# Half products of the first two feature tiles with the first 256 rows from 32-bit operands, row tiles 0 and 1 normalised one by one, and dues set anew, in a spectral filter with a gated feed-forward

## The chip, the cores and the metric

The kernel runs on one core of a Trainium2 chip. The metric is the device time of one execution in microseconds. The engines are PE (matrix products), DVE and ACT (elementwise work), POOL (some elementwise work) and SP, which issues the DMAs. Each engine runs its own instructions in program order; semaphores connect them.

## The reference

```
xn = (x - mean(x)) / sqrt(var(x) + 1e-5)              # x: 2048 x 512
s  = irfft2(rfft2(xn) * (w_r + 1j * w_i))             # w: 2048 x 257
gate, up = xn @ W_gate, xn @ W_up                     # W: 512 x 1376
h  = gate * (gate > 0) * up
g  = silu(h @ W_down)                                 # 1376 x 512
out = x + s * g
```

## The kernel before

**Numbers.** Every 32-bit operand is split into two f16 halves, high and low. A product is three passes over them (`PASSES`: high·high, high·low, low·high), summed in PSUM. So that the halves keep their precision, each weight tile is first scaled by a power of two: ACT squares it and sums along the rows, PE adds over the partitions with a matrix of ones (`group_scale`, into the PSUM tile `small` for groups 0 and 1, into a tile `sum` for the others), DVE makes the scale `p`, and ACT and DVE write the halves `wgu` (`group_split`).

**Tiles.** The 2048 rows are 16 row tiles of 128, taken in pairs c (x0 is row tiles 0 and 1, x1 is 2 and 3), and four blocks of 512 rows for the feed-forward. The 1376 features are 11 feature tiles f, the last of 96. They are loaded in the groups `GROUPS`: f = 0, 1 and 2 alone, then two by two. The raw 32-bit weights of group g are `raw{g}_0` (gate) and `raw{g}_1` (up).

**The feed-forward.** For each block and each f, `product` makes the gate and the up sums (`gu`) of 512 rows: 12 matmuls each (four parts of 128 inputs by three passes). `rectify` makes `r` (ACT, Relu), `hidden` multiplies by the up sums (DVE) and splits the result into the halves `h16`. `down` multiplies them by the split down weights `wds` into `dn`; the scale of these hangs on all weight tiles. `down_scale`: the sums of the raw down weights (ACT) times `rho`, the inverse scales of all groups, give `md`; DVE reduces it, SP writes the 128 results to DRAM as one row (`row_md`) and reads the row back to all partitions (`rows_md`), DVE takes the greatest (`max_md`) and makes the scales `scd`. `down_weights` then makes the halves f by f. The f16 pair of f is written in the place of the raw tile of f − 1, so the high half of f + 1 (ACT) waits for the low half of f (DVE).

**The opening.** The first 512 rows are turned by PE instead of by DMA (`turn_row`): four transposes per row tile into `head` (PSUM), the high half of `xT` by ACT, the low half by DVE. For f = 0 and 1 (`HALF`) of block 0 the product is made in two halves of 256 rows, so that rows 0 to 255 can begin before rows 256 to 511 are there. `keep_busy` puts dummy matmuls of ones into `small` until then.

**The filter.** The two-dimensional transform is done as stages of small matrix products: the first stage `s` per pair of row tiles (with `xs`, folded rows), its result written to DRAM, read back by chunks q, the middle stages `y`, `xx`, `z`, `v`, the filter's weights between `xx` and `z`, DRAM again, and a last stage. These stand on PE between the products of the feed-forward.

**The order.** No order is written out. `Plan` collects steps, each with an engine, a planned cost, what it reads and writes, and for some a due time; dues are handed back to what a step depends on. `Plan.run` then lists the steps by its own clock: of those that can begin, each engine takes the one with the earliest due. The instructions are put out in that order. The numbers at the top of the file set the dues: of the feed-forward through a running clock (`tick`, from `T0`), of the stages by a start and a step (`FIRST`, `MID`, `LAST`), of the down weights by `DOWN`. So a changed number can move work far from where it is used.

Of the kernel before, what the change touches and what calls it, by code (L numbers as in the profile page):

```python
# [14 lines left out]
P = 128  # L15
# [14 lines left out]

T0, DOWN, FIRST, FIRST_STEP, MID, MID_STEP, LAST, LAST_STEP = 1.2, 94.9, 53.3, 17.6, 150.3, 18.1, 292.6, 10.8
LOADS, LOADX = [4.2, 0, 4.4, None, None, None, None], [-2.7, -0.3]
FOLDS, FOLD_LEAD, MARGIN = ['DVE', 'DVE', 'DVE', 'DVE', 'DVE', 'DVE', 'DVE', 'DVE'], 67.8, 1.95
# [5 lines left out]
HURRY, SLOW, SLOW_TO = -2, 1, 20  # L41
LOWS = [("DVE", "DVE")] * 8


RANGES = ((0, 257, 0), (257, 512, 1))
# [189 lines left out]
def kernel(ctx: ExitStack, tc: tile.TileContext, x, wg, wu, wd, wl, ew, sp, c_r, c_d, c_m, c_x, c_s, out):  # L235
# [37 lines left out]
    POOL.memset(unit, 0.0)  # L273
    POOL.affine_select(out=unit, in_=unit, compare_op=ALU.not_equal, fill=1.0, base=0, pattern=[[-1, P]], channel_multiplier=1)
    warm = cpool.tile([P, 1], F32, name="warm")
    ACT.activation(warm, ones[:, 0:1], AF.Sqrt)
    DVE.memset(md, 0.0)

# [23 lines left out]
    def load_x(c):  # L302
        tile_of(f"x{c}", "k4", [P, 2, D], F32)
        if c == 1:
            after_first(("x1", 0), lambda: T["x1"][:, 0, 0:1])
        for i in range(1 + (c == 0)):
            rows = slice(i, i + 1) if c == 0 else slice(0, 2)
            step("SP", .5, lambda rows=rows: SP.dma_start(T[f"x{c}"][:, rows], x[:, 2 * c + rows.start:2 * c + rows.stop, :]),
                 writes=[(f"x{c}", i)], lead=14 if c else None, kb=256 * (rows.stop - rows.start), lag=2.2, due=(LOADX[c] + i * .01) if c < 2 else None)

    def x_names(c, i):
        return [(f"x{c}", 0 if c else i)]
# [1 line left out]
    def stats(c, q, j):  # L314

        def run(i):
            st = T[f"st{c}"][:, 6 * i:6 * i + 6]
            DVE.bn_stats(st, T[f"x{c}"][:, i, :])
            DVE.bn_aggr(T[f"mv{c}"][:, i, :], st)
        tile_of(f"st{c}", "q", [P, 12], F32)  # L320
        tile_of(f"mv{c}", "mv", [P, 2, 2], F32)
        for i in range(2):
            step("DVE", .82, lambda i=i: run(i), reads=x_names(c, i), writes=[(f"st{c}", i), (f"mv{c}", i)])

    def deviation(c):

        tile_of(f"q{c}", "q", [P, 4, 2], F32)

        def first():
            q = T[f"q{c}"]  # L330
            DVE.tensor_scalar(q[:, 0], T[f"mv{c}"][:, :, 1], EPS, -4.0 / XS ** 2, op0=ALU.add, op1=ALU.mult)

        def last():
            ve, sq, y, t = (T[f"q{c}"][:, i, :] for i in range(4))
            DVE.reciprocal(y, sq)
            for i in range(2):
                DVE.scalar_tensor_tensor(t[:, i:i + 1], y[:, i:i + 1], ve[:, i:i + 1], y[:, i:i + 1],
                                         op0=ALU.mult, op1=ALU.mult)
            DVE.scalar_tensor_tensor(y, t, 3.0, y, op0=ALU.add, op1=ALU.mult)
            if "ACT" in NORM[c]:  # L340
                DVE.scalar_tensor_tensor(ve, T[f"mv{c}"][:, :, 0], -1.0, y, op0=ALU.mult, op1=ALU.mult)
        step("DVE", .13, first, reads=[(f"mv{c}", 0), (f"mv{c}", 1)], writes=[f"q{c}"], port=True)
        step("ACT", .11, lambda: ACT.activation(T[f"q{c}"][:, 1], T[f"q{c}"][:, 0], AF.Sqrt, scale=-1.0),
             reads=[f"q{c}"], writes=[(f"q{c}", 1)])
        step("DVE", .78 + .14 * ("ACT" in NORM[c]), last, reads=[(f"q{c}", 1)], writes=[(f"q{c}", 2)], port=True)
        return f"q{c}", 0

    def deviations(cs):

# [16 lines left out]
    def normalise(c, q, at, engines=("DVE", "DVE")):  # L366

        tile_of(f"xf{c}", "k4", [P, 2, D + 2], F32)

        def run(i):  # L370
            to, x = T[f"xf{c}"][:, i, 0:D], T[f"x{c}"][:, i, :]
            if engines[i] == "ACT":
                ACT.activation(to, x, AF.Identity, bias=T[q][:, 0, i:i + 1], scale=at()[:, i:i + 1])
            else:
                DVE.tensor_scalar(to, x, T[f"mv{c}"][:, i, 0:1], at()[:, i:i + 1], op0=ALU.subtract, op1=ALU.mult)
        for i in range(2):
            e = engines[i]
            step(e, .62 if e == "ACT" else dve2(512), lambda i=i: run(i), reads=[*x_names(c, i), (f"mv{c}", i), (q, 2)],
                 writes=[(f"xf{c}", i)], port=e == "DVE")

    def turn(c, lows):
# [24 lines left out]
    def turn_row(c, i):  # L406

        if (c % 2, i) == (0, 0):
            tile_of(f"xT{c // 2}", "xg", [P, 4, 8, P], F16)
        if i == 0:  # L410
            tile_of(f"head{c}", "F", [P, 2, D], F32)
        j = 2 * (c % 2) + i
        head = lambda: T[f"head{c}"][:, i, :]
        xt = lambda h: T[f"xT{c // 2}"][:, j, 4 * h:4 * h + 4].rearrange("p k r -> p (k r)")

        def run():
            for k in range(4):
                cols = slice(k * P, k * P + P)
                PE.transpose(head()[:, cols], T[f"xf{c}"][:, i, cols], unit)
        step("PE", .45, run, reads=[(f"xf{c}", i)], writes=[(f"head{c}", i)])  # L420
# [66 lines left out]
    def load_group(g):  # L487
        w = sum(fwidth(f) for f in GROUPS[g])
        for i, src in enumerate((wg, wu)):
            tile_of(f"raw{g}_{i}", "k4", [P, 4, w], F32)  # L490
            if g == 1 and not i:
                after_first("raw1_0", lambda: T["raw1_0"][:, 0, 0:1])
            of = src[:, 4 * P * GROUPS[g][0]:4 * (P * GROUPS[g][0] + w)].rearrange("p (k f) -> p k f", k=4)
            step("SP", .5, lambda i=i, of=of: SP.dma_start(T[f"raw{g}_{i}"], of),
                 reads=["go"] if g else [], writes=[f"raw{g}_{i}"], lead=12 if g else None, kb=2 * w, lag=2.5, due=LOADS[g])

    def squares(g):
        tile_of(f"m{g}", "m", [P, 4], F32)
# [7 lines left out]

    def group_scale(g):
        nf = len(GROUPS[g])
        if g > 1:
            tile_of(f"sum{g}", "F", [P, 4], F32)  # L510
        to, name = ((lambda: T[f"sum{g}"]), f"sum{g}") if g > 1 else ((lambda: T["small"][:, 4 * g:4 * g + 4]), ("small", g))
# [3 lines left out]
        step("DVE", .52, lambda: scale_of(to()[:, :2 * nf], T[f"p{g}"][:, :, :2 * nf], 9), reads=[name], writes=[f"p{g}"], port=True)  # L515

    def group_split(g):
        fs = GROUPS[g]
# [144 lines left out]

    def tick(cost):
        t = clock[0]
        clock[0] += cost * (SLOW if cost < 2 and t < SLOW_TO else 1.0 if t < 60 else 1.17)
        return t

    def product(c, f, i, rows=slice(0, 4), tag="gu"):
# [10 lines left out]
                tile_of(name, tag, [P, 2, 4, P], F32)  # L680
        elif name not in T.tiles:
            tile_of(name, tag, [P, 4, P], F32)

        def run():
            t, xT = T[name][:, i] if tag == "F" else T[name], T[f"xT{c}"]
# [19 lines left out]
    def rectify(c, f):  # L705
        e, n = fwidth(f), f"r{c}_{f}"
        G, names = sums[c, f, 0]
        tile_of(n, "k2", [P, 4, P], F32)
        step("ACT", act(512), lambda: ACT.activation(T[n][:e], G()[:e], AF.Relu, scale=2.0 ** -22), reads=names, writes=[n], due=clock[0] + 3)

    def hidden(c, f):
# [5 lines left out]
        if f == TAIL:  # L717
            def run():
                for s in range(2):
                    DVE.tensor_mul(h32()[:64, 2 * s:2 * s + 2], up()[64 * s:64 * s + 64, 0:2], r()[:64, 2 * s:2 * s + 2])  # L720
                DVE.tensor_mul(h32()[64:e], gate()[96:], r()[64:e])
            step("DVE", 1.6, run, reads=[*G, *U, f"r{c}_{f}"], writes=[n32], due=clock[0] + 3)
        else:
            step("DVE", dve(512), lambda: DVE.tensor_mul(h32(), up(), r()), reads=[*U, f"r{c}_{f}"], writes=[n32], due=clock[0] + 3)
        step("ACT", act(512), lambda: ACT.activation(h16()[:e, 0], h32()[:e], AF.Copy), reads=[n32], writes=[(n16, 0)])
# [294 lines left out]
    for c in range(NCH):  # L1020
# [7 lines left out]
        for k in [c] if c < 2 else [c - 1, c] if c % 2 else []:  # L1028
# [8 lines left out]
    filter_scale(MID - 12)  # L1037
    for h in range(2):
        for f in range(HALF):
            for i in range(2):  # L1040
                product(0, f, i, slice(2 * h, 2 * h + 2), ("gu", "dn", "F")[f])
            if h:
                rectify(0, f)
                hidden(0, f)
# [12 lines left out]
        ff_steps(c)  # L1057
    for q in range(NCH):
        T.within(f"mid{q}", "mid")
        fft_chunk(q, [MID + MID_STEP * q + k for k in (0, 5, 15, 20)])  # L1060
    T.within(None, None)
    for c in range(NCH):
        last_stage(c, LAST + LAST_STEP * (c | PAIR2))
    for c in range(NCH):
        for i in range(2):
            finish(c, i, LAST + 10 + LAST_STEP * c if c < 6 else clock[0] + 8)
    T.run()


# [120 lines left out]
```

## Time and profile before

| | |
|---|---|
| median of 3 runs | 409.06 us (409.02 to 409.29) |
| span of the profiled execution | 407.1 us |
| PE busy | 401.4 us (99%) |
| DVE busy | 304.0 us (75%) |
| ACT busy | 188.0 us (46%) |
| POOL busy | 46.7 us (11%) |
| granted PE clock | 1.000 |

The profiler saw one execution; of that one the span, from the first to the last instruction, is what it gives for its time. The timed runs have some 2 us more around it. Nearly all records bear the line of one helper (L65 before, L73 after), so groups are told apart by the names of tiles: `gu<-xT,wgu` is a product of the feed-forward, `dn<-wds,h` a down product. A row of the timeline has its start, its busy time, the engine, the line, the operation, out<-in, and how many instructions it gathers.

### The profile page before, as it was taken

What the parts mean: (1) busy time and instruction counts of PE and PEld (TensorE: products, weight loads), DVE (VectorE), ACT (ScalarE), POOL (GpSimd) and SP (SyncE); (2) the same over time, 40 slices, a digit from 0 to 9 for tenths busy, and PEclk for the clock granted to TensorE, in tenths of its full rate; (3) what the DMA queues carried; (4) which work ended last, traced back from release to release, by engine and by line L of the source; (5) the groups of instructions that cost most, each with busy time, mean ns of one, the idle gap of its engine ahead of it and who ended that gap; (6) DMA issues with size and microseconds to landing.
All of it is one profiled execution on the core that took longest, in us unless ns stands there. A gap on an engine that the chain in (4) does not pass through costs nothing.

```text
span 407.1 us, 7606 instructions
## 1 busy us (share of the span) xinstructions
PE 401.4 (99%) x2992; PEld 211.5 (52%) x2992; DVE 304.0 (75%) x647; ACT 188.0 (46%) x358; POOL 46.7 (11%) x72
## 2 busy tenths in 40 slices
PE   8999999999999999999999999999999999999995
PEld 7864444444444445455465455546555444444555
DVE  4897986998798979706987578686792328987974
ACT  4999823743467636222355433534523336242411
POOL 0000000000000000001612032030330008040300
PEclk9999999999999999999999999999999999999999
DMA  7980002218549608690006540324201297563242
GB/s 244 403 304 1 0 2 109 54 52 208 171 152 305 172 15 209 128 291 13 2 0 191 173 144 0 100 92 149 52 2 52 61 242 182 161 185 105 103 156 103
DMA packets 36291, 51.78 MB, mean 127 GB/s; under 512 B 15840, under 2 KB 17600, under 8 KB 36256
## 3 DMA queue, kind: packets, MB, share of 16 engines
q1 hardware_dynamic: 36256, 51.31, 42.5%
q8 instruction: 23, 0.38, 0.4%
q14 instruction: 12, 0.10, 0.1%
HBM read 35.55 MB, written 12.60 MB: 118 GB/s over the span
## 4 chain that ended last, share of the span: by engine, by line
PE 97%; ACT 1%; DVE 1%; issue 0%
PE gu L65 55%; PE dn L65 27%; PE s L65 3%; PE z L65 3%; PE xx L65 3%; PE small L65 2%; PE y L65 2%; PE v L65 2%; PE dn_3b L65 1%; ACT xT L65 1%; ACT wgu L65 0%; PE head L65 0%; DVE xT L65 0%; PE sum L65 0%; DVE p L65 0%
## 5 line engine op out<-in xcount | busy, mean ns | idle before, releaser
L65 PE MATMUL gu<-xT,wgu 128*128 128x512 f16 (+1 forms) x1008 | 213.3, 369 | 0.4 <-DVE xT L65 0.4
L65 PEld LDWEIGHTS <-wgu 128*128 128x128 f16 x1008 | 97.5, 98 | 107.5 <-issue 3.5
L65 PE MATMUL dn<-wds,h 128*128 128x512 f16 (+2 forms) x528 | 115.8, 373 | 0.0
L65 PEld LDWEIGHTS <-h 128*128 128x128 f16 (+1 forms) x561 | 53.7, 98 | 57.3 <-issue 2.0
L65 DVE TENSOR_TENSOR h<-gu,r 128x512 f32<-128x512 f32 (+2 forms) x52 | 33.6, 646 | 24.2 <-PE gu L65 22.9
L65 ACT ACTIVATE h<-h 128x512 f16<-128x512 f32 (+1 forms) x44 | 27.5, 626 | 51.0 <-DVE h L65 51.0
L65 POOL TENSOR_TENSOR po<-tt,tt 128x256 f32<-128x256 f32 x16 | 14.4, 900 | 262.6 <-DVE tt L65 208.7
L65 ACT ACTIVATE r<-gu 128x512 f32<-128x512 f32 (+1 forms) x44 | 26.2, 595 | 36.5 <-PE gu L65 36.3
L65 DVE TENSOR_TENSOR h<-h,h 128x512 f16<-128x512 f32 (+1 forms) x44 | 29.7, 689 | 5.3 <-ACT h L65 5.1
L65 DVE SCALAR_TENSOR_TENSOR tt<-xsp,cw,wt 128x512 f32<-128x512 f32 x32 | 25.3, 847 | 0.0
L65 POOL TENSOR_TENSOR ae<-zz 128x128 f32<-128x128 f32 (+1 forms) x32 | 17.8, 593 | 62.8 <-ACT zz L65 47.9
L65 ACT ACTIVATE g<-dn,cdi 128x512 f32<-128x512 f32 (+1 forms) x16 | 10.6, 673 | 23.9 <-PE dn L65 23.9
L65 PE MATMUL gu<-xT,wgt 128*64 128x256 f16 (+1 forms) x144 | 17.0, 309 | 0.0
L65 DVE TENSOR_TENSOR sv<-sv,g 128x512 f32<-128x512 f32 (+1 forms) x17 | 11.2, 690 | 6.4 <-ACT g L65 6.1
L65 DVE TENSOR_TENSOR t<-v,t 128x1024 f16<-128x1024 f32 x8 | 9.8, 1219 | 7.9 <-ACT t L65 7.9
L65 DVE TENSOR_TENSOR z<-z,z 128x1024 f16<-128x1024 f32 x8 | 9.7, 1218 | 7.5 <-ACT z L65 7.5
L65 ACT ACTIVATE z<-z 128x1024 f16<-128x1024 f32 x8 | 8.2, 1024 | 15.2 <-PE z L65 15.2
L65 POOL TENSOR_TENSOR pf<-tt,tt 128x256 f32<-128x256 f32 x16 | 14.0, 888 | 7.7 <-PE gu L65 7.7
L65 ACT ACTIVATE p<-pf 128x1024 f16<-128x1024 f32 x8 | 8.4, 1056 | 13.0 <-DVE pf L65 13.0
L65 DVE SCALAR_TENSOR_TENSOR wgu<-raw,p,wgu 128x512 f16<-128x512 f32 x20 | 14.4, 745 | 0.1
L65 ACT ACTIVATE xs<-xs 128x1024 f16<-128x1024 f32 x8 | 8.3, 1052 | 12.8 <-DVE xs L65 9.3
L65 ACT ACTIVATE wgu<-raw 128x512 f16<-128x512 f32 x20 | 12.3, 619 | 3.7 <-DMA raw<-in_wg 3.7
(134 smaller groups left out, 430.6 us busy)
## 6 DMA issues: line engine op xcount, KB each, us to landing
A_d<-t SPq DMA_DIRECT2D x16, 256.0 KB, 3.3
rw<-in_wl SPq DMA_DIRECT2D x8, 512.0 KB, 5.1
wt<-in_wl SPq DMA_DIRECT2D x8, 512.0 KB, 4.8
at<-A_d SPq DMA_DIRECT2D x8, 512.0 KB, 4.9
C_d<-t SPq DMA_DIRECT2D x16, 256.0 KB, 3.3
ct<-C_d SPq DMA_DIRECT2D x16, 256.0 KB, 5.6
xt<-in_x SPq DMA_DIRECT2D x16, 256.0 KB, 4.3
out<-xt SPq DMA_DIRECT2D x15, 256.0 KB, 2.1
```

The costliest lines, as they stand in the source:

```text
L65: return lambda *args, **kw: self.tc.keep_in_program_order(f(*args, **kw))
```

## The change

The change has these parts:

- **Row tiles 0 and 1.** `deviation` and `normalise` of pair 0 treat the two row tiles one by one (`ALONE`). The statistics of row tile 1 are made by ACT (a sum, a scaling, a sum of squares) and one DVE multiplication.
- **Transposed rows.** For pair 0 the `head` is first copied as 32-bit numbers to `xTf0` (ACT) and `xTf1` (DVE); the halves of `xT` are made from these copies.
- **32-bit half products.** For f < 2 and rows 0 to 255, `product` multiplies the raw weights by `xTf`: per row tile and part of 128 inputs one matmul of 128 columns, 32 matmuls in all, instead of 48 f16 matmuls of 256 columns. These sums are not scaled, so `rectify` and `hidden` treat the two halves of such a tile apart, with the scale `p` and a new tile `ups` for the first.
- **PSUM.** Group 2 sums its squares into `small`; the second feature tile's halves use a tile of the tag `F`.
- **Dues.** `BUSY` goes from 79 to 42 dummies; the starts and steps of the stages become lists; loads, squares and folds get other leads.

```
-BUSY, LATE, PAIR1, PAIR2 = 79, 0.4, 0, 0
-SQUARES, HALF = 32.82, 2
+BUSY, LATE = 42, 0.4
+SQUARES, HALF = 32.321, 2
+ALONE, EVAC, WHOLE = (((0,), (1,)), ((0, 1),)), ("ACT", "DVE"), .95
+HALVES, HEADS, STATS = ('gu', 'F'), [None, 8.91], ((0, 1),)
...
+            if (c, i) in STATS:
...
+                step("ACT", .75, lambda: ACT.activation(junk(), of(), AF.Copy, accum_out=st()[:, 6:7]),
...
+                step("ACT", .2, lambda: ACT.activation(st()[:, 7:8], st()[:, 6:7], AF.Copy, scale=-1.0 / D),
...
+                step("ACT", .8, lambda: ACT.activation(junk(), of(), AF.Square, bias=st()[:, 7:8], accum_out=st()[:, 8:9]),
...
+                step("DVE", .13, lambda: DVE.tensor_scalar(mv()[:, i, :], st()[:, 6:9:2], 1.0 / D, None, op0=ALU.mult),
...
+        if c == 0:
+            n = f"xTf{i}"
+            tile_of(n, "k2", [P, 4, P], F32)
...
+            step(e, (dve if e == "DVE" else act)(512), act_ if e == "ACT" else lambda: DVE.tensor_copy(T[n].rearrange("p k r -> p (k r)"), head()),
...
+            step("ACT", act(512), lambda: ACT.activation(xt(0), of(), AF.Copy), reads=[n], writes=[(f"xT{c // 2}", j, 0)])
+            step("DVE", dve(512), lambda: DVE.tensor_sub(xt(1), of(), xt(0)), reads=[n, (f"xT{c // 2}", j, 0)],
...
+        if c == 0 and f < HALF and rows.start == 0:
+            def whole(j):
+                for k in range(4):
+                    matmul(to()[:, j], T[f"raw{g}_{i}"][:, k, :], T[f"xTf{j}"][:, k, :], start=k == 0, stop=k == 3)
+            for j in range(2):
+                step("PE", WHOLE, lambda j=j: whole(j), reads=[f"xTf{j}", f"raw{g}_{i}"], writes=[(name, 0, i)], due=tick(WHOLE))
...
+            for k, by in enumerate((lambda: T[f"p{f}"][:, 0, 0:1], lambda: 2.0 ** -22)):
+                at = slice(2 * k, 2 * k + 2)
+                step("ACT", act(256), lambda at=at, by=by: ACT.activation(T[n][:, at], G()[:, at], AF.Relu, scale=by()),
...
-            first_stage(k, FIRST + FIRST_STEP * (k | PAIR1))
+            first_stage(k, FIRSTS[k])
...
-        fft_chunk(q, [MID + MID_STEP * q + k for k in (0, 5, 15, 20)])
+        fft_chunk(q, [MIDS[q] + k for k in STAGES])
```

The order on PE in the opening, before: the two row tiles are turned together (`head`, eight transposes), dummies follow, then the sum for the scale of a weight group (`m,ones`), and the first f16 half product.

```order
L65 MATMUL small<-ones 128x256
L65 MATMUL head_214<-unit,xf_201 128x128 x8
L65 LDWEIGHTS ones
L65 MATMUL small<-ones 128x256
...
L65 MATMUL small<-m_251,ones 128x2
...
L65 LDWEIGHTS wgu_77
L65 MATMUL gu_0_0_274<-xT_233,wgu_77 128x256
```

After, at the same place; row tile 0 was turned a little ahead, and the first row here is the last dummy before the products.

```order
L73 MATMUL small<-ones 128x256
L73 MATMUL gu_0_0_218<-xTf_209,raw_0_129 128x128 x4
L73 MATMUL gu_0_1_231<-xTf_209,raw_1_134 128x128 x4
L73 MATMUL head_197<-unit,xf_157 128x128 x4
L73 MATMUL gu_1_245<-xTf_209,raw_0_153 128x128 x4
L73 MATMUL small<-m_189,ones 128x2
L73 MATMUL gu_0_0_218<-xTf_251,raw_0_129 128x128 x4
...
L73 MATMUL head_293<-unit,xf_274 128x128 x8
L73 MATMUL gu_1_245<-xTf_209,raw_1_166 128x128 x4
...
L73 LDWEIGHTS wgu_77
L73 MATMUL gu_0_0_218<-xT_267,wgu_77 128x256
```

The half products of rows 0 to 255 now stand ahead of the weight sums and the first `wgu`, two of the eight groups even ahead of the turning of row tile 1; the turning of rows 256 to 511 (eight transposes) stands behind six of them.

The order on DVE around the reduction of `md`, before. `p` and `rho` belong to the last weight groups, `h_0_6` is the multiplication in `hidden` of block 0, f = 6, which reads the up sums `gu_6_1`.

```order
L65 SCALAR_TENSOR_TENSOR rho<-p_686 128x2
L65 TENSOR_SCALAR wgu_82<-raw_1_393,p_659 128x4x128
L65 TENSOR_TENSOR md<-md,rho 128x11
L65 TENSOR_REDUCE md<-md 128x1
L65 SCALAR_TENSOR_TENSOR wgu_82<-raw_1_393,p_659,wgu_82 128x4x128
L65 SCALAR_TENSOR_TENSOR wgu_83<-raw_0_485,p_686,wgu_83 128x512
L65 TENSOR_SCALAR wgu_83<-raw_1_489,p_686 128x512
L65 TENSOR_SCALAR wgt<-raw_1_489,p_686 128x4x32
L65 TENSOR_TENSOR h_0_6_754<-gu_6_1_719,r_6_732 128x512
```

After:

```order
L73 SCALAR_TENSOR_TENSOR wgu_82<-raw_0_432,p_676,wgu_82 128x4x128
L73 TENSOR_TENSOR h_0_6_704<-gu_6_1_661,r_6_674 128x512
L73 TENSOR_SCALAR p_706<-sum_689 128x4
L73 TENSOR_SCALAR p_706<-p_706 128x4 x2
L73 SCALAR_TENSOR_TENSOR wgu_82<-raw_0_432,p_676,wgu_82 128x4x128
L73 TENSOR_SCALAR p_706<-p_706 128x4
L73 SCALAR_TENSOR_TENSOR rho<-p_706 128x2
L73 TENSOR_SCALAR wgu_82<-raw_1_438,p_676 128x4x128
L73 TENSOR_TENSOR md<-md,rho 128x11
L73 TENSOR_REDUCE md<-md 128x1
L73 SCALAR_TENSOR_TENSOR wgu_82<-raw_1_438,p_676,wgu_82 128x4x128
```

The scale of the last group, and with it the reduction of `md`, stood five places ahead of `h_0_6`; it now stands eight behind it.

On PE the new order leaves the products for a stage of the filter 35 times over the whole program, where the order before did so 41 times, since more chunks are taken two by two.

More of the change, by code (lines that the diff above doesn't have):

```diff
@@ L275 @@
     warm = cpool.tile([P, 1], F32, name="warm")
+    ups = cpool.tile([P, HALF], F32, name="ups")
     ACT.activation(warm, ones[:, 0:1], AF.Sqrt)
@@ L308, in load_x @@
             step("SP", .5, lambda rows=rows: SP.dma_start(T[f"x{c}"][:, rows], x[:, 2 * c + rows.start:2 * c + rows.stop, :]),
-                 writes=[(f"x{c}", i)], lead=14 if c else None, kb=256 * (rows.stop - rows.start), lag=2.2, due=(LOADX[c] + i * .01) if c < 2 else None)
+                 writes=[(f"x{c}", i)], lead=14 if c else None, kb=256 * (rows.stop - rows.start), lag=2.2, due=(LOADX[c] + i * .1) if c < 2 else None)
     def x_names(c, i):
@@ L327, in deviation @@
         tile_of(f"q{c}", "q", [P, 4, 2], F32)
[L329 to L341, printed above, removed]
@@ L665, in tick @@
         t = clock[0]
-        clock[0] += cost * (SLOW if cost < 2 and t < SLOW_TO else 1.0 if t < 60 else 1.17)
+        clock[0] += cost * (SLOW if cost < 2 and t < SLOW_TO else 1.0 if t < 60 else TICK)
         return t
@@ L682, in product @@
             tile_of(name, tag, [P, 4, P], F32)
+        to = lambda: T[name][:, i] if tag == "F" else T[name]
+        if c == 0 and f < HALF and rows.start == 0:
[4 more added lines that the diff above has]
+                step("PE", WHOLE, lambda j=j: whole(j), reads=[f"xTf{j}", f"raw{g}_{i}"], writes=[(name, 0, i)], due=tick(WHOLE))
+            sums[c, f, i] = to, [(name, k, i) for k in range(2)]
+            return
         def run():
```

82 lines of the change are left out of this document (63 added, 19 removed).

## Prediction

> **What bounds the kernel now.** I read the page first, then PE's waits, the chain of waits, and the timeline of the two stretches that the change touches. From the page, the span and busy time by engine:
>
> ```profile
> span 407.1 us, 7606 instructions
> PE 401.4 (99%) x2992; PEld 211.5 (52%) x2992; DVE 304.0 (75%) x647; ACT 188.0 (46%) x358; POOL 46.7 (11%) x72
> ```
>
> PE is busy all the time. So the time is PE's work, what it does while it has nothing better, and a fixed rest. From PE's waits (engine and group, released by: us, times, longest) and, below, the chain of waits (start, us, what):
>
> ```profile
> PE small L65 <- DVE md L65: 1.1, 1, 1.1
> PE gu L65 <- DVE xT L65: 0.4, 1, 0.4
> ...
> 1.05 7.58 PE small L65 x47
> 20.10 0.69 DVE xT L65
> 20.83 18.24 PE gu L65 x107
> 400.39 2.64 PE dn_3b L65 x24
> ```
>
> The last wait ends at 20.83: the low halves of row tiles 2 and 3, made by DVE until 20.79, come too late for PE. From 20.83 to 403.03 (400.39 + 2.64) PE waits for nothing. Hence two rules for the sum: what brings the products of rows 256 to 511 forward from 20.83 is gained in full, and any wait that appears behind it is lost in full. The median, 409.06, is 2.0 us above the span; I carry differences over to it.
>
> The opening, from the timeline (start, us, engine, operation, count):
>
> ```profile
> 3.49 0.69 DVE L65 BATCH_NORM_STATS2 st<-x 128x6 f32<-128x512 f32 x1 [2.47 <-DMA x<-in_x]
> 7.46 0.38 PE L65 MATMUL small<-m,ones 128*128 128x2 f32 x2
> 7.45 0.30 PEld L65 LDWEIGHTS small<-m,ones 128*128 128x128 f32 x2 [0.27 <-ACT wgu L65]
> 7.70 0.92 PE L65 MATMUL small<-ones 128*128 128x256 f16 x7
> 9.33 2.78 PE L65 MATMUL small<-ones 128*128 128x256 f16 x24
> 9.89 1.07 ACT L65 ACTIVATE xT<-head 128x512 f16<-128x512 f32 x2
> 12.69 2.78 PE L65 MATMUL gu<-xT,wgu 128*128 128x256 f16 x24
> 15.45 0.82 ACT L65 ACTIVATE xf<-x,q 128x512 f32<-128x512 f32 x1
> 17.30 1.04 PE L65 MATMUL head<-unit,xf 128*128 128x128 f32 x8
> 17.19 0.91 PEld L65 LDWEIGHTS head<-unit,xf 128*128 128x128 f32 x8
> 18.17 0.38 PE L65 MATMUL small<-ones 128*128 128x256 f16 x2
> ```
>
> The real products start only at 12.69, since the f16 weights need a scale (the sum on PE at 7.46, then DVE and ACT). PE passes the time with dummies, 79 in all. Eight heads take .87 us (17.30 to 18.17), .109 each, with eight 32-bit weight loads beside them.
>
> **The change part by part.** *32-bit products.* They replace 48 f16 half products. An f16 one of 128x256 takes (15.47 − 12.85)/24 = .109 us by the chain:
>
> ```profile
> 12.85 2.62 PE gu L65 x24
> 15.47 0.12 PE sum L65 x2
> ```
>
> so 5.2 us go. Each 32-bit matmul is two records (7.46, x2 for one). No row has one that moves 128 columns; the nearest are the heads, 128 columns of 32 bits in .109 per record. Two records make .217, and 32 of them 6.9 us. The upper end is the small matmul, which moves almost nothing and still holds PE for 7.70 − 7.46 = .24, its weight load: .245 each, 7.8 us. I take .217, as the moving operand is like the heads'. So PE's work grows by 1.7 us (2.6 at the upper end). What is bought is the earlier start: raw weights need no scale, and half of the work needs only one row tile.
>
> When do they start? Row 0 goes alone. Its statistics start at 3.49, and with .18 for the aggregate and some 1.7 us for the scale, with no weights on ACT before it, its normalised row is ready at about 6.7. PE's 37 dummies last to 7.2 (38 to 7.46 here), the four heads to 7.7 and the copy of 512 columns on ACT to 8.4. From 8.46 PE has eight groups of four (6.9), four and eight heads (1.3) and two sums (.5): ready for the next rows at 17.2, or 18.1 at .245.
>
> The other bound is DVE and ACT. Here row 3's normalisation starts on ACT at 15.45 and the heads at 17.19, after the halves; from the heads' start to 20.83 it is 3.5 us. In the new order the eight heads stand behind six groups: 8.46 + 5.2 + .4 + .25 = 14.3. Adding 3.5 gives 17.85; going through ACT's and DVE's new order by the same durations gives 17.45. ACT's three statistics passes on row 1 (from its landing to 5.9, before the first weights) cost nothing there, and DVE's extra ops of .16 us are inside that chain. I take 17.6: **−3.2 us** (bounds −3.4 and −2.3, the latter with .245). If this cover fails, PE simply waits as it does today.
>
> *Later weight groups.* With PE 3.2 us ahead, ACT and DVE must deliver the f16 halves of f = 1 to 8 earlier too. Going through their new order by the durations of this stretch, f = 1 and 2 come some .1 us ahead of PE and f = 7 some .7 us: no wait, but thin. I put 0, with +.7 as the upper end.
>
> *Down weights.* This is where the gain is paid back. Timeline rows of the chain from md to the last scaled down weight:
>
> ```profile
> 50.03 0.16 DVE L65 TENSOR_REDUCE md<-md 128x1 f32<-128x11 f32 x1
> 52.63 0.69 DVE L65 TENSOR_TENSOR h<-gu,r 128x512 f32<-128x512 f32 x1 [0.52 <-PE gu L65]
> 50.22 0.33 SPq L65 DMA_DIRECT2D row_md<-md  x1
> 59.47 0.32 SPq L65 DMA_DIRECT2D rows_md<-row_md  x1
> 64.45 0.29 DVE L65 TENSOR_REDUCE max_md<-rows_md 128x1 f32<-128x128 f32 x1 [4.16 <-DMA rows_md<-row_md]
> 65.34 0.23 DVE L65 TENSOR_SCALAR scd<-rho,pd 128x11 f32<-128x11 f32 x1
> 65.61 0.72 ACT L65 ACTIVATE wds<-wds,scd 128x512 f16<-128x512 f32 x1 [4.62 <-DVE scd L65]
> 67.22 0.74 DVE L65 SCALAR_TENSOR_TENSOR wds<-wds,scd 128x512 f16<-128x512 f32 x1
> 84.59 0.75 DVE L65 SCALAR_TENSOR_TENSOR wds<-wds,scd 96x512 f16<-96x512 f32 x1
> 73.63 27.30 PE dn L65 x126
> 141.09 0.33 SPq L65 DMA_DIRECT2D row_mw<-mw  x1
> 148.39 0.32 SPq L65 DMA_DIRECT2D rows_mw<-row_mw  x1
> ```
>
> The reduction of md now stands behind h of f = 6 on DVE, with some 2.9 us of its own neighbours between. That h is at 52.63 here, at 49.4 when PE is 3.2 earlier, so the reduction ends near 52.35 instead of 50.19: 2.15 later, although all of PE is earlier. From there to scd it is 15.4 us (50.19 to 65.57), mostly one tiny row written (50.22 to 59.47, 9.25) and read back. So scd is at about 67.7. The down products start at 73.63 − 3.2, near 70.5: the lead shrinks from 8.1 to 2.8 us. The scaled weights leave one by one: each high half on ACT waits for the low half of the one before, at least .72 + .74 + .07 = 1.53 us, while PE eats one in six matmuls of .217, 1.30. They are no longer far enough ahead. Going through the new order I find small waits at f = 3 to 10 that sum to 2.6 us. In the trace the eleven take 17.4 us (67.22 to 84.59); at that pace f = 10 would come 4.1 us late, the upper end. Behind a down product that waits stand all later ones of these rows and the products of the next block, so each wait is lost in full. The written row isn't a constant: the same kind for mw took 7.3 (141.09 to 148.39), and with that the waits sum to .7. I take the mean of the two rows, 8.3, and **+1.6 us** (bounds 0 and +4.1).
>
> *Stage visits.* In the new order PE leaves the products for a filter stage 35 times, not 41. A pair of first stages and a single one, by the chain:
>
> ```profile
> 68.06 1.44 PE s L65 x48
> 100.94 0.78 PE s L65 x24
> ```
>
> Two singles are 1.56, so a visit costs .12: six give **−.7 us**, between −.7 and 0 if some partner isn't ready.
>
> *The rest.* Fewer dummies (42) matter only in the opening, where they are counted above. Splitting rectify and hidden for f < 2 adds two ACT and two DVE calls off PE's path. Dues of the middle and last stages move; the shortest distances of PE between dependent stages stay within .5 us of today's. I put 0, with +1.5 as the upper end.
>
> Sum: −3.2 + 1.6 − .7 = −2.3, hence 409.06 − 2.3 = **406.8 us**.
>
> **The rivals.** *A, no wait at the down weights.* The row takes 7.3 us or less and ACT and DVE run the chain at 1.53. For it: the mw row. Against: md is 2.15 later and the lead is 2.8. Then −3.2 − .7 = −3.9, 405.2 us.
>
> *B, slower: 32-bit weight loads are not hidden.* Every one of the 32 matmuls brings a new stationary operand of 32 bits, loaded twice, and the row at 7.45 has two loads in .30 us. If loads and matmuls alternate, one costs .217 + .30 = .52, 32 of them 16.5 instead of 6.9, and PE is ready at 26.8, 6.0 after today's 20.83; the down weights then keep their lead: +6.0 − .7 = +5.3, 414.4 us. It decides from about .35 us a matmul, where (.35 − .217) · 32 = 4.3 uses up today's start and the .7. For it: the sum at 7.46 holds PE .24 with two moving columns. Against: eight 32-bit loads lie under eight heads in .87 us. The Trainium skill, "TensorE: Matmul & The Clock Gate", section "The mechanism", says that a weight load overlaps a running matmul only where the row groups differ; all of these use the same 128 rows, so by that rule B would hold and the time would be its 414.4 us. The heads here, 128 rows after 128 rows at .109, speak against the rule. Its section "Weight-path perf modes" adds that the fast weight load isn't given to 32-bit operands, which no row here contradicts.
>
> *C, the down weights at the trace's own pace.* The row takes 9.25 or more and DVE puts other work between the low halves as it does here: +4.1 in place of +1.6, 409.3 us, no gain.
>
> *D, a new wait in the filter stages.* First stages are paired earlier and middles moved: one chunk late by 1 to 2 us gives 408 to 409.5. Against: distances on PE hardly change.
>
> That the change doesn't do what it says is excluded by the order, where the 32-bit products stand.
>
> **How the numbers follow.** Forecast 406.8 (about 405.9 to 408.2): .45. A: .20. B: .10. C: .13. D: .12. Differences under 0.2%, .8 us, are about what a measurement of this kernel can't tell from no change. Faster (below 408.24): the forecast, A and some of D, .69. Within: the rest of D and a part of C, .13. Slower: B, the rest of C, .18. The range, 405.2 to 409.5, leaves out B and half of A's lower side.
>
> **What would show it.** In the changed profile: the first 32-bit product near 8.5 and the first f16 product of rows 256 to 511 near 17.6 (right), 32-bit records at .109 (B if the spacing is over .17); md's reduction near 52.3, scd near 67.7, PE waits named by wds of 1 to 3 us between 70 and 90; and rows of s and y in longer pairs. I am wrong if PE's products start after 20, if wds shows no wait or over 4 us, or if waits named by xs, at or ct show up later.

## The result: 418.34 us, slower by 2.3%

The changed kernel takes 418.34 us (417.75 to 419.70, 4 runs) against 409.04 us before (408.80 to 409.29, 4 runs): ratio 1.0234, 95% interval 1.0218 to 1.0250. The forecast was 406.8 us with 409.5 as its upper end. The profiled execution of the changed kernel took 418.41 us with a span of 416.6 (407.1 before).

The page of the changed kernel, span, busy time and granted clock in 40 slices:

```profile
span 416.6 us, 7570 instructions
PE 401.2 (96%) x2971; PEld 212.3 (51%) x2971; DVE 305.1 (73%) x654; ACT 190.3 (46%) x367; POOL 47.6 (11%) x72
PEclk9999999999999999987999999999999999999999
```

PE is busy as long as before (401.2 against 401.4) and the span is 9.5 us longer: the loss is waiting, and in slices 18 and 19 a lower clock. PE's waits name it (engine and group, released by: us, times, longest):

```profile
PE y L73 <- DMA at<-A_d: 5.4, 1, 5.4
PE gu L73 <- DVE h L73: 2.2, 2, 1.6
PE dn L73 <- DVE wds L73: 1.5, 3, 0.7
...
PE gu L73 <- DVE xT L73: 0.8, 1, 0.8
```

The chain of waits, for the start of the second halves, the wait for `h` right behind it, the place of the longest wait (`at`, the first middle stage's input, read back from DRAM), and the end:

```profile
17.96 2.67 PE gu L73 x23
...
22.11 0.49 DVE h L73
...
22.65 1.48 PE gu L73 x12
...
176.45 4.17 DMA A_d<-t
...
180.68 5.66 DMA at<-A_d
...
186.39 3.47 PE y L73 x105
189.86 3.81 PE dn L73 x12
...
409.96 2.64 PE dn_3b L73 x24
```

In the kernel before, the chain has the same 105 records of `y` as

```profile
180.84 1.99 PE y L65 x105
```

and twelve down products take 2.59 (12 × .216). Here they take 3.47 and 3.81, 2.7 us more. Busy time and granted clock of the changed kernel in stretches of 2 us (start:end, length, PE busy, clock, DMA share, GB/s) show why:

```profile
180.00:182.00 2.00, 0.97 (x5) 1.00 0.75 70
182.00:184.00 2.00, 0.00 (x0) 1.00 0.93 281
184.00:186.00 2.00, 0.00 (x0) 0.81 1.01 376
186.00:188.00 2.00, 1.61 (x46) 0.50 0.98 380
190.00:192.00 2.00, 2.00 (x6) 0.50 0.00 0
192.00:194.00 2.00, 2.00 (x36) 0.98 0.00 0
```

In this run the clock is halved after some 4 us of waiting and comes back only after some 6 us of work: the wait of 5.4 us costs 8.1.

The account, from the starts of successive matmuls against their usual distance: the second halves start at 17.96 instead of 20.83, −2.9; the half products of f = 1 wait once more, for `h`, +.7; seven steps of the first down products come late, +2.9; `h` is late near 157, +1.7; `at` and the half clock, +8.1; the remainder, put down to fewer stage visits, −1.0. Sum +9.5; PE's last matmul ends at 412.60 (409.96 + 2.64) instead of 403.03, +9.6.

### The profile page after: what moved, and what is told of

The parts are those of the page before. It is cut to its first block, busy times and chain, and to the rows that moved or that the text cites. A ratio compares the mean times of both kernels' runs of the same rounds, so it can differ in the third digit from the quotient of the medians.

```text
span 416.6 us, 7570 instructions
## 1 busy us (share of the span) xinstructions
PE 401.2 (96%) x2971; PEld 212.3 (51%) x2971; DVE 305.1 (73%) x654; ACT 190.3 (46%) x367; POOL 47.6 (11%) x72
## 4 chain that ended last, share of the span: by engine, by line
PE 73%; DVE 12%; DMA 10%; ACT 3%; issue 1%; SPq 1%; POOL 0%; DVEq 0%
PE gu L73 39%; PE dn L73 21%; DVE h L73 3%; PE z L73 3%; PE xx L73 3%; PE s L73 2%; DMA row_md<-md 2%; DVE wgu L73 2%; PE y L73 2%; DMA xT<-x 2%; DVE wds L73 2%; DVE xs L73 2%; PE v L73 2%; DMA raw<-in_wg 1%; DMA at<-A_d 1%; DMA rows_md<-row_md 1%
## 5 line engine op out<-in xcount | busy, mean ns | idle before, releaser
L73 PE MATMUL gu<-xT,wgu 128*128 128x512 f16 (+1 forms) x960 | 208.3, 374 | 2.9 <-DVE h L73 2.2
L73 PEld LDWEIGHTS <-wgu 128*128 128x128 f16 x960 | 92.9, 98 | 109.9 <-issue 6.2
L73 PE MATMUL dn<-wds,h 128*128 128x512 f16 (+2 forms) x528 | 118.2, 375 | 1.8 <-DVE wds L73 1.5
L73 PEld LDWEIGHTS <-h 128*128 128x128 f16 (+1 forms) x561 | 54.1, 98 | 60.9 <-issue 6.9
L73 DVE TENSOR_TENSOR h<-gu,r 128x512 f32<-128x512 f32 (+3 forms) x52 | 33.1, 636 | 29.2 <-PE gu L73 27.8
L73 ACT ACTIVATE r<-gu 128x512 f32<-128x512 f32 (+2 forms) x44 | 25.7, 584 | 47.2 <-PE gu L73 47.1
L73 POOL TENSOR_TENSOR po<-tt,tt 128x256 f32<-128x256 f32 x16 | 14.6, 915 | 281.7 <-DVE tt L73 235.2
L73 ACT ACTIVATE h<-h 128x512 f16<-128x512 f32 (+1 forms) x44 | 27.3, 624 | 40.5 <-DVE h L73 40.3
L73 DVE TENSOR_TENSOR h<-h,h 128x512 f16<-128x512 f32 (+1 forms) x44 | 30.3, 696 | 7.3 <-ACT h L73 7.1
L73 POOL TENSOR_TENSOR ae<-zz 128x128 f32<-128x128 f32 (+1 forms) x32 | 20.0, 659 | 62.9 <-ACT zz L73 62.8
L73 DVE SCALAR_TENSOR_TENSOR tt<-xsp,cw,wt 128x512 f32<-128x512 f32 x32 | 26.1, 878 | 0.0
L73 ACT ACTIVATE g<-dn,cdi 128x512 f32<-128x512 f32 (+1 forms) x16 | 10.6, 672 | 30.0 <-PE dn L73 30.0
L73 DVE TENSOR_TENSOR z<-z,z 128x1024 f16<-128x1024 f32 x8 | 9.7, 1221 | 10.6 <-ACT z L73 10.6
L73 PE MATMUL gu<-xT,wgt 128*64 128x256 f16 (+1 forms) x144 | 17.0, 309 | 0.0
L73 ACT ACTIVATE a<-y 128x1024 f16<-128x1024 f32 x8 | 8.1, 1022 | 18.4 <-PE y L73 18.3
L73 DVE TENSOR_TENSOR a<-y,a 128x1024 f16<-128x1024 f32 x8 | 9.8, 1220 | 8.5 <-ACT a L73 8.5
L73 DVE TENSOR_TENSOR sv<-sv,g 128x512 f32<-128x512 f32 (+1 forms) x17 | 11.5, 709 | 5.3 <-ACT g L73 5.1
L73 DVE SCALAR_TENSOR_TENSOR wgu<-raw,p,wgu 128x512 f16<-128x512 f32 x20 | 14.2, 746 | 0.9 <-ACT wgu L73 0.9
L73 ACT ACTIVATE xs<-xs 128x1024 f16<-128x1024 f32 x8 | 8.3, 1053 | 13.1 <-DVE xs L73 13.1
L73 ACT ACTIVATE t<-v 128x1024 f16<-128x1024 f32 x8 | 8.1, 1022 | 13.1 <-PE v L73 13.1
L73 DVE TENSOR_TENSOR t<-v,t 128x1024 f16<-128x1024 f32 x8 | 9.7, 1222 | 5.9 <-ACT t L73 5.9
L73 PE MATMUL y<-cm,at 64*128 64x64 f16 x384 | 8.3, 202 | 5.4 <-DMA at<-A_d 5.4
```

Source lines behind the costliest of these rows:

```text
L73: return lambda *args, **kw: self.tc.keep_in_program_order(f(*args, **kw))
```

## The experiments

Runs e1 to e8, f2 and f3 move single steps in a kernel's finished order and leave every other instruction where it was; in f1, f4, g1 to g3 and h1 the planner set the order anew from other numbers. What stood on SP ahead of the read of `at` (timeline: start, us, operation, count), first before, with DVE taking up what was read, then after:

```profile
165.49 2.99 SPq L65 DMA_DIRECT2D A_d<-t  x4
168.53 6.72 SPq L65 DMA_TRANSPOSE xT<-x  x2
175.45 1.54 SPq L65 DMA_DIRECT2D at<-A_d  x3
179.75 0.20 DVE L65 COPY am<-at 128x126 f16<-128x126 f16 x1 [6.83 <-DMA at<-A_d]
```

```profile
162.41 0.35 SPq L73 DMA_DIRECT2D row_mw<-mw  x1
...
164.25 9.90 SPq L73 DMA_TRANSPOSE xT<-x  x1
174.25 3.19 SPq L73 DMA_DIRECT2D A_d<-t  x4
...
180.68 1.55 SPq L73 DMA_DIRECT2D at<-A_d  x3
```

Two differences strike the eye: a turning DMA (DMA_TRANSPOSE) of 9.9 us ahead of the writes, and the tiny write `row_mw`, which before stood at 141.

**Theory 1: SP's order of turning DMA and writes.** Run e1 puts the writes ahead in the changed kernel; run e4 puts them behind in the kernel before.

```diff
# e1, SP of the changed kernel          # e4, SP of the kernel before
-DMA_TRANSPOSE xT<-x_7                  +DMA_TRANSPOSE xT<-x_6
 DMA A_d<-t_6 x2                        +DMA_TRANSPOSE xT<-x_7
 DMA A_d<-t_7 x2                         DMA A_d<-t_6 x2
+DMA_TRANSPOSE xT<-x_7                   DMA A_d<-t_7 x2
 DMA rows_mw<-row_mw                    -DMA_TRANSPOSE xT<-x_6, x_7
```

> The changed kernel with one move on SP: the turning DMA of row pair 7 (xT<-x) goes behind the four writes A_d<-t of row pairs 6 and 7; nothing else moves. Theory 1 (SP's order makes the first middle stage late): the writes go out near 167.2 when DVE has made t, not at 174.25; the read at<-A_d follows near 177, lands near 182.5, and PE's wait for at falls from 5.4 to 1 to 2.5 us, with no half clock behind it; 418.3 becomes 411.5 to 413.5. Theory 2 (the data are late anyway: the first stages stand 2 us later and the DMA engines are full): the wait stays over 3.5 us, 416 or more.

> The kernel before with one move on SP: the four writes A_d<-t of row pairs 6 and 7 go behind the two turning DMAs of the same pairs. Theory 1: the turning DMAs start near 168.5 as now and hold SP until 175.3; the writes follow, the read near 182, and PE, which is at the first middle stage at 180.8, waits 5 to 7 us and then runs at half clock for some us: 409.0 becomes 416 to 419, the whole loss of the change by one move. Theory 2 (SP's order is not what decides): 411 or less.

Both fail theory 1. e1: 418.31 us, ratio 1.0231 (1.0210 to 1.0253), and PE waits 6.0 us for `at`. e4: 409.18 us, ratio 1.0014 (1.0004 to 1.0023). SP's timeline of e1 and of e4:

```profile
166.90 3.10 SPq L73 DMA_DIRECT2D A_d<-t  x4
170.05 7.86 SPq L73 DMA_TRANSPOSE xT<-x  x1
180.17 1.92 SPq L73 DMA_DIRECT2D at<-A_d  x3
```

```profile
165.49 4.51 SPq L65 DMA_TRANSPOSE xT<-x  x2
170.06 3.63 SPq L65 DMA_DIRECT2D A_d<-t  x4
176.53 1.43 SPq L65 DMA_DIRECT2D at<-A_d  x3
```

In e1 the writes go out 7 us earlier and the read no earlier, as the turning DMA now holds SP for 7.9 us behind them; the writes themselves are slow too, up to 9.2 us until they have landed. In e4 two turning DMAs take 4.5 us together. In the kernel before this order is harmless; something in the changed kernel makes the DMAs slow.

**The down weights.** e2 moves the sums of the last two weight groups and md's reduction together to the last sum of the raw down weights; e3 adds the move of e1.

```diff
 PE:  gu_5_0
+PE:  sum 5, sum 6                (from behind gu_6_0 and gu_6_1)
 DVE: xs<-eo x2
+DVE: p 5, rho 5, p 6, rho 6, md<-md,rho, TENSOR_REDUCE md
```

> The changed kernel with the sums of the last two weight groups (PE), their scales, rho and the reduction of md (DVE) moved together to where the last sum of the raw down weights is made; nothing else moves. Theory 1 (the waits for wds, 2.9 us, come from the late md): md's reduction ends near 46 and not 53.4, scd comes at 61 to 62, no wait for wds is left. If the later waits stayed as they are, 415.4; as PE comes 2.9 us earlier to a read that SP's order sets, the wait for at may grow by as much, so 415.4 to 418.3. Theory 2 (ACT and DVE can't make the halves faster in this order): the waits for wds stay over 1.5 us.

> The changed kernel with both moves of the two runs before. Theory 1: no wait for wds, at's wait 1 to 4 us as PE is earlier, no or little half clock: 409 to 412. Theory 2: 414 or more.

e2: 419.45 us, ratio 1.0255 (1.0214 to 1.0296). No wait for wds is left, but this does not show that md's place alone caused it. DVE now stands 1.6 us for the sums and spends 2.3 us on twelve small operations ahead of the weight halves, PE waits 2.0 us for `wgu`, and so it comes to the down products only at 73.98, where the change was there at 71.51; `scd` is ready at 66.6, 2.2 us earlier than in the change, not at 61 to 62. The wait for `at` stays at 5.0:

```profile
PE y L73 <- DMA at<-A_d: 5.0, 1, 5.0
...
PE gu L73 <- DVE wgu L73: 2.0, 2, 1.8
```

e3: 417.17 us (414.63 to 418.46), ratio 1.0195 (1.0156 to 1.0234). Theory 1's range for e3 failed. Its profiled execution is the fastest of the four; there PE waits 3.0 us for `at`, as the turning DMA holds SP for 6.2 us and the read goes out at 178.0, while the waits for `wgu` have taken the place of those for wds.

**What makes the turning DMA slow.** e5 puts `row_mw` behind it, e6 puts the reads directly behind the writes, e7 takes two loads of the filter's weights from ahead of the turning DMA of pair 5, e8 joins e6, e7 and an earlier md.

```diff
# e5                       # e6                        # e7
-DMA row_mw<-mw            -DMA_TRANSPOSE xT<-x_7      +DMA_TRANSPOSE xT<-x_5
 DMA cm, wt<-in_wl          DMA A_d<-t_6 x2, t_7 x2     DMA rw<-in_wl
 DMA_TRANSPOSE xT<-x_7     +DMA at<-A_d x3              DMA rw<-in_wl
+DMA row_mw<-mw            +DMA_TRANSPOSE xT<-x_7      -DMA_TRANSPOSE xT<-x_5
 DMA A_d<-t_6 x2, t_7 x2    DMA rows_mw<-row_mw
```

> The changed kernel with one move on SP: the tiny write row_mw<-mw goes behind the turning DMA of row pair 7 (so it is issued after it and just ahead of the writes A_d<-t). Theory 3 (a turning DMA is slow while the element-wise write of row_mw is under way): the turning DMA takes 3 to 4 us instead of 9.9, the writes go out near 168, and at's wait falls below 3 us: 411 to 414. Theory 4 (it is slow because of the 512 KB of filter weights that are issued just ahead of it, wt<-in_wl): it stays at 8 to 10 us and the time at 417 to 419.

> The changed kernel with the three reads at<-A_d directly behind the four writes A_d<-t on SP, and the turning DMA of row pair 7 behind them; what else stood between stays behind. Theory 5 (not the writes alone but everything on SP between t and the read, the turning DMA above all, sets when at lands): the writes go out near 167, the read near 173 when they have landed, at lands near 178.5, before PE is there at 180.6: no wait for at, no half clock, 8 us less: 409 to 411. Theory 2 (the data are late by themselves): a wait over 3 us stays, 415 or more. A later wait for xT (row pair 7) or for the filter's weights would show as a new line of PE's waits.

> The changed kernel with one move on SP: the last two loads rw<-in_wl go behind the turning DMA of row pair 5. If PE's wait for h near 156.5 (1.6 us) comes from DVE, which waits 4.0 us for the buffer that this slow turning DMA still reads, then the turning DMA takes 3 us, DVE's and PE's waits vanish. As the wait for at is set by SP behind it, it may grow by what is won: 416.5 to 418.5 in all. Rival: the turning DMA stays at 6 to 8 us and nothing changes.

> The changed kernel with three moves: the reads of at directly behind the writes of A_d (as in the run before last), the last two loads rw behind the turning DMA of row pair 5, and the sum of the last weight group on PE beside that of the one before, with its scale and the reduction of md ahead of h of f = 6 on DVE. If all losses of the change are these waits: 418.3 less 8.1 (at and half clock), 1.7 (h) and 1.5 to 2.9 (wds): 405.6 to 407, below the kernel before by the opening's 2.9 us. Rival: new waits take their place, 409 or more.

e5: 420.26 us, ratio 1.0280 (1.0251 to 1.0310), no gain, and yet its trace decides. First SP's timeline, then the chain of waits:

```profile
164.45 2.76 SPq L73 DMA_TRANSPOSE xT<-x  x1
167.27 0.57 SPq L73 DMA_DIRECT2D row_mw<-mw  x1
167.93 3.06 SPq L73 DMA_DIRECT2D A_d<-t  x4
```

```profile
169.95 12.38 DMA A_d<-t
```

Without `row_mw` ahead of it the turning DMA takes 2.8 us, not 9.9, as theory 3 had it; the filter weights (theory 4) still stand ahead of it. But the writes, now right behind `row_mw`, take 12.4 us to land, where they took 4.2 in the change. The 512 bytes delay whatever is queued next.

e6: 422.66 us, ratio 1.0335 (1.0316 to 1.0354). The read does follow the writes, but the last of these, issued 6.7 us behind `row_mw`, takes 8.4 us (`170.27 8.37` in its chain), and PE waits 8.8 us for `am`, a DVE operation that stands behind DVE's wait for `rows_mw`. Theory 5 alone is not enough. e7: 416.66 us, ratio 1.0196 (1.0170 to 1.0221): the turning DMA of pair 5 stays at 5.7 us, so that the loads ahead didn't slow it, but it begins 1.8 us earlier; the wait for `h` near 157 goes, and one of 1.3 us for ACT's `r` takes its place. e8: 419.67 us, ratio 1.0267 (1.0240 to 1.0293), with 8.0 us for `am` as in e6 and .6 us for wds. Its three moves gained nothing while `row_mw` stood where it stood.

**Theory 6: the place of `row_mw`.** Its due is one number, FILTER. f1 sets it back in the changed kernel; g2 sets it forward in the kernel before.

```diff
# f1, changed kernel                   # g2, kernel before
-FILTER = 153.189                      -    filter_scale(MID - 12)
+FILTER = 138.3                        +    filter_scale(153.189)
```

> The changed kernel with one number as it was before: FILTER = 138.3 (the due of the tiny write row_mw, of the squares of the filter weights and of their loads) instead of 153.189; the planner then sets the order anew, with row_mw some 20 us ahead of the last writes A_d<-t. Theory 6 (a DMA that is queued behind the element-wise row_mw lands only when that has drained, 8 to 9 us; in the change it stands right ahead of the turning DMA, the writes of A_d and the read): the writes land 3 to 5 us after their issue, at's wait is under 2 us, and 418.3 becomes 408 to 412. Theory 2 (the data are late because the first stages stand later): 415 or more.

> The kernel before with one number of the change: the due of row_mw is 153.189 instead of 138.3, all else as it was; the planner then issues the loads of the filter weights later and puts row_mw just ahead of the reads of at, behind the last writes A_d<-t. Theory 6: the read at<-A_d is held by row_mw for some 8 us, PE waits 3 to 7 us for at and runs at half clock behind it: 409 becomes 413 to 418. Theory 2 (only the later first stages and shorter distances of the change make it): under 411.

f1: 410.93 us, ratio 1.0049 (1.0036 to 1.0062): one number takes 7.4 of 9.3 us away. `row_mw` goes out at 142.6, and PE no longer waits for `at`; it waits most for wds now:

```profile
PE dn L73 <- DVE wds L73: 1.7, 3, 0.9
```

g2: 422.59 us, ratio 1.0331 (1.0315 to 1.0346): the same number, alone, makes the kernel before 13.8 us slower, more than theory 6 had expected. SP's timeline, the chain and PE's waits of g2:

```profile
177.55 0.52 SPq L65 DMA_DIRECT2D row_mw<-mw  x1
179.41 5.52 SPq L65 DMA_DIRECT2D at<-A_d  x3
```

```profile
179.41 13.42 DMA at<-A_d
```

```profile
PE y L65 <- DMA at<-A_d: 11.8, 1, 11.8
```

The read, issued 1.9 us behind `row_mw`, lands after 13.4 us. FILTER also sets the dues of the loads `rw`, and in g2 four of them stand ahead of a turning DMA that takes 8.2 us; so not all of the 13.8 is `row_mw`. That the place of these steps decides, and not the later first stages of theory 2, is shown from both sides.

f2 and f3 leave FILTER and move `row_mw` and its read behind the reads of `at`, the operations that wait for it on DVE behind two middle chunks; f3 adds the moves of e8.

> The changed kernel with the write row_mw and its read back behind the three reads of at on SP, and the greatest of them and the filter's scale on DVE behind the splitting of the first two middle chunks, so that nobody waits for them early; the rest stands as in the change. Theory 6: the turning DMA of row pair 7 takes under 4 us, the writes go out near 167.5 and land by 174, the read goes out at 174 to 176 and lands near 181: a wait for at of at most 1.5 us and no half clock, 410 to 412. Theory 2: the wait stays over 4 us. If the filter's scale is now late, a wait for z will show it.

> As the run before, and with the turning DMA of row pair 7 behind the reads of at, the last two loads rw behind the turning DMA of row pair 5, and md's reduction ahead of h of f = 6 (as in the run with three moves, where it left .6 us of waits for wds). Theory 6: no wait for at, waits of 1 to 2 us elsewhere: 405.5 to 407.5, below the kernel before by the opening's gain. Rival: 409 or more, new waits.

f2: 414.11 us, ratio 1.0118 (1.0101 to 1.0135); f3: 415.80 us, ratio 1.0173 (1.0149 to 1.0198). The mechanism held and the price moved. From f3's chain and PE's waits:

```profile
166.53 3.79 DMA A_d<-t
```

```profile
PE y L73 <- issue: 2.7, 1, 2.7
PE xx L73 <- DVE a L73: 1.1, 1, 1.1
```

The writes land in 3.8 us (4.1 in f2) and no wait for `at` is left in either. In f2 nothing but `row_mw` and its readers was moved, so it is `row_mw` that held up `at`. But `row_mw` now lands near 187, and the filter's scale, with the later chunks behind it on DVE, is late: PE waits 3.1 us at `xx` in f2 and 1.1 in f3, with a halved clock behind. The 2.7 us at `y` in f3 have no releaser in the profile; their cause is open.

**What is left, and what the opening is worth.** g1 adds to f1 the sum of the last group beside that of the one before and md's reduction ahead of `h` of f = 6. h1 adds to g1 the reads of `at` ahead of both turning DMAs.

> The changed kernel with FILTER = 138.3 as before, and the sum of the last weight group on PE beside that of the one before, with its scale and md's reduction ahead of h of f = 6 on DVE. If the 2 us that the run with FILTER alone still lost are the waits for wds (1.7 us by the waits, some 2.9 with the doubled steps beside them): 408 to 409. If ACT's and DVE's chain is the limit and not md: 410.5 to 411.

> The run with FILTER = 138.3 and md's reduction early, and now the two turning DMAs of row pairs 6 and 7 behind the three reads of at on SP. In that run at landed at 182.63 and PE took it up at 182.68, so that any delay of a DMA was lost, and its times spread from 408.8 to 412.5. If that is the cause, at lands near 180, the times draw together at 408 to 409, at or a little below the kernel before. If the spread has another cause it stays.

g1: 410.48 us (408.81 to 412.49, 9 runs), ratio 1.0043 (1.0024 to 1.0062). h1: 409.53 us (408.93 to 412.67, 11 runs), ratio 1.0024 (1.0008 to 1.0040). In g1 waits for wds fall to .7 us in the profiled execution, but the median is above the 408 to 409 that was expected, and no gain over f1 is clear of noise. h1's median is .9 lower still, with intervals that overlap and one run of 412.67, so that neither a gain nor the cause of the spread is shown. It is the best of the changed kernels, and none beats the kernel before. In h1 the second halves start at 18.48, 2.4 us ahead of the kernel before, but by the starts of successive matmuls .7 is lost again at `h` of f = 1 and 2.0 at the down products.

f4 keeps the new opening and takes the old dues; g3 keeps the new dues with FILTER = 138.3 and makes rows 0 to 255 of f = 0 and 1 from f16 halves.

```diff
# f4                                        # g3
-FIRSTS = [58.53, 65.2, 93.07, ...]         -        if c == 0 and f < HALF and rows.start == 0:
+FIRSTS = [53.3 + 17.6 * k for k ...]       +        if False and f < HALF and rows.start == 0:
 (T0, MIDS, STAGES, LASTS, ENDS, DOWN,       (rectify, hidden likewise; BUSY = 79)
  FILTER, folds and squares likewise)
```

> The parts of the change that touch the opening (32-bit half products, row tiles one by one, statistics on ACT, 42 dummies) with the dues of the kernel before for the stages, the down weights and the filter (two values of the loads stay as in the change); the planner sets the order. On PE the opening reads as in the change. If the opening's gain of 2.9 us is real and only the dues lost it: 405 to 408. If the opening itself makes the later stretches wait (the down weights come closer, the first stages must follow an earlier PE): 408 to 412.

> The changed kernel with FILTER = 138.3 and without the 32-bit half products: rows 0 to 255 of f = 0 and 1 from f16 halves as before, rectify and hidden in one piece, 79 dummies; row tiles still one by one, other dues as in the change. It is to be compared with the run with FILTER alone (410.9). If the 32-bit products bring PE 2.9 us forward and 2 of them are lost to waits for wds: 411 to 413 here, with the first f16 product of rows 256 to 511 near 20.5 and less wait for wds. If they bring nothing: 410 to 411.

f4: 414.58 us, ratio 1.0136 (1.0120 to 1.0152), above both of its ranges. The second halves begin at 18.4 and nothing waits for `at`, but the down weights are late by more than in the change, and the clock halves there. PE's timeline and its clock:

```profile
74.47 0.38 PE L73 MATMUL dn<-wds,h 128*128 128x512 f16 x1 [2.31 <-ACT wds L73]
75.31 4.87 PE L73 MATMUL dn<-wds,h 128*128 128x512 f16 x14 [0.46 <-DVE wds L73]
```

```profile
76.00:78.00 2.00, 2.00 (x6) 0.50 0.57 117
```

g3: 414.82 us, ratio 1.0154 (1.0133 to 1.0175), also above both of its ranges and 3.9 us slower than f1, which differs by the 32-bit products, the dummies that go with them and the order that follows. Its chain has `23.56 18.24 PE gu L73 x107`: without them the rest begins at 23.56. Not all of the 3.9 is the opening: PE also waits once 2.3 us for `h`, where f1 waits .6. Still, f16 halves in this opening start the rest 2.7 us later than the kernel before did (20.83), and the 32-bit products some 3 us earlier (17.69 in f1): at that point they have paid for the 1.7 us of work that they add, though no kernel here keeps the gain to its end.

## Why the prediction was wrong

**The opening** was right. The second halves start at 17.96 (forecast 17.6), and 32-bit records follow at .112. From the timeline of the changed kernel, sixteen records and the sum behind them:

```profile
14.98 1.95 PE L73 MATMUL gu<-xTf,raw 128*128 128x128 f32 x16
16.77 0.28 PE L73 MATMUL small<-m,ones 128*128 128x2 f32 x2
```

(16.77 − 14.98)/16 = .112, so that rival B is out: weight loads of 32 bits lie under the matmuls here as under the heads. This is against the rule of the Trainium skill, "TensorE: Matmul & The Clock Gate", section "The mechanism", which lets a load overlap only with matmuls on other row groups, though the same section also has loads pulled ahead into a background weight buffer; every record here uses all 128 rows, and the measurement decides.

**Later weight groups** were put at 0, and PE waits for no `wgu`: right. The .7 us lost at 22.65 only look like the upper end of this term. They are a wait that the sum did not have: the up products of rows 256 to 511 of f = 1 begin when `hidden`'s multiplication (`22.11 0.49 DVE h`) has ended, and both work on the one PSUM tile that f = 1 now has (tag `F`). The prediction had put the splitting of `hidden` off PE's path.

**The down weights** were the right mechanism, mis-sized: +2.9 measured where +1.6 was put. The rows behind it, from the timeline and from the chain of waits:

```profile
53.26 0.17 DVE L73 TENSOR_REDUCE md<-md 128x1 f32<-128x11 f32 x1
68.54 0.23 DVE L73 TENSOR_SCALAR scd<-rho,pd 128x11 f32<-128x11 f32 x1
```

```profile
53.45 8.96 DMA row_md<-md
```

md's reduction ends at 53.4 (52.35 forecast), scd at 68.8 (67.7). The tiny write took 8.96, near the 9.25 of the same transfer before; the mean with `row_mw` was the wrong choice, and the 2.6 worked out with 9.25 was nearly it. How much of it is md's place shows in g1 against f1: scd is ready .9 us earlier (67.9, 68.7), and the late steps fall from 3.2 to 2.0 us. The rest is the pace of the scaled halves, 1.54 us each where PE needs 1.30.

**Stage visits** came out at −1.0 for −.7, as the remainder of the account and not by a measurement of their own. The 41 and 35 visits count stages, some of which follow one another directly: by PE's records it left the products 35 and 33 times.

**"The rest", put at 0 with +1.5 as the upper end, is the step that failed.** It weighed the shifted dues by distances on PE alone, and held that these stayed within .5 us. This failed twice. From the last first stage ahead of it to the first middle stage PE's own work is shorter: the stage ends at 162.48 and PE is ready for `y` at 181.0, 18.5 us, where it was 20.4 (160.41 to 180.84) with the read taken up by DVE at 179.75, only 1.1 us ahead. And what is queued on SP in that stretch did not enter the sum at all: FILTER had moved `row_mw` from 141 to 162, right ahead of the turning DMA, the writes and the read. The price was on the table, as the prediction itself quoted that write with 7.3 us; PE lost nothing behind it before, so it looked like a constant of another chain. Rival D named the kind of loss at 1 to 2 us; it was 9.8 (`at` 5.5 from the starts of the matmuls, the clock 2.6, `h` 1.7). `row_mw` accounts for `at` and the clock behind it; the wait for `h` stays when `row_mw` alone is moved (f2, 1.9) and gives way to one of 1.3 us for `r` when two loads of the filter's weights, which FILTER sets too, are moved (e7). The prediction's own sign of being wrong, a wait named by `at`, showed up. No term of the sum had a lower clock, as waits before were under 1.2 us.

## What to carry to other kernels

When dues move, follow each DMA to its queue: what stands ahead of it there now, and who needs what stands behind it. A slow transfer that nobody waits for is cheap only while nothing that is needed soon stands behind it in its queue. And a wait of several us on PE costs more than itself, since the clock must be earned back.

## What the runs showed of the hardware

A write of 128 single elements (512 bytes) takes 7.0 to 10.3 us to land where its landing is on record (e4, g2; 7.3 before, 8.3 in the change), and DMAs queued behind it wait with it: the writes `A_d<-t` landed after 12.4 us right behind it (e5), 8.4 us when issued 6.7 us behind it (e6), 3.8 us without it (f3); a turning DMA held SP for 9.9 and 11.2 us behind it (the change, e7) and for 2.8 without (e5). It is not the only thing that slows a turning DMA: behind the reads of `at` one held SP for 5.8 us (f3).

The clock halves and comes back in steps. If it is either 1 or .5 within a stretch, the means give the time of each turn: .81 in 184 to 186 and .98 in 192 to 194 make 6.8 us of half clock in the change, .97 in 74 to 76 and .68 in 78 to 80 make 3.4 in f4, .51 in 184 to 186 and .57 in 196 to 198 make 13.7 in g2, all whole multiples of 3.4. So where a pause lies may count as much as its length; that is an inference, and no run here moves a pause alone. The pauses that were followed by half clock were 2.7 us and more within some 3 us (2.3 and .5 in f4, 2.7 in f3, 3.0 in e3); one of 2.3 us left the clock at 1.00 (`h` near 157 in e2, e5 and g3). The Trainium skill, "TensorE: Matmul & The Clock Gate", section "What's actually happening", has an idle window of about 3.4 us for this. The step of 3.4 us agrees with it, but a pause shorter than the window was enough in f3, f4 and e3, so there the measurement decides.
